# DMA transposes of whole tiles: one request for four blocks of 128 columns in place of four requests

## The chip, the cores and the metric

One core of a Trainium2 chip (trn2). The metric is the device time of one execution in microseconds (us). "Faster" or "slower" means by more than 2%.

## The reference, cut to what matters

The input x is 2048 rows of 512 columns. It is normalised by rows, goes through a local attention of 32 heads and, in parallel, through a gated MLP; the two results are multiplied and added to x.

```python
xn = _layernorm(x, axis=-1)                       # (1, 2048, 512)
s = _A_ref(xn, A_wqkv, A_wo)                      # xn @ wqkv (512 x 1536), attention, @ wo
g = _silu(_B_ref(xn, B_w_gate, B_w_up, B_w_down)) # 512 -> 1792 -> 512
return x + s * g
```

All first products contract over the 512 columns of xn, and the kernel's matmuls read xn with its columns on the partitions: each 128 x 512 tile of xn has to be transposed into four blocks of 128 x 128.

## The kernel before

The rows come in four stages of 512 (`TQ`), each of four tiles (`TPQ`). The first five tiles are transposed by TensorE; the other eleven by DMA, issued on SyncE (`nc.sync`), 44 requests of one block each:

```python
    def transpose_by_dma(t, cs=range(NC)):          # NC = 4 blocks in a tile
        j, i = divmod(t, TPQ)
        if i == 0 and 0 in cs:
            xnT[j] = xtp.tile([P, NC, TQ], BF16, name="xnT")
        for c in cs:
            nc.sync.dma_start(
                out=xnT[j][:, c, i * P : (i + 1) * P],
                in_=xns[t][:, c * P : (c + 1) * P],
                transpose=True,
            )

    def project(ps, w, lo, j, i0=0, n=TQ):          # who reads xnT
        for dk in range(NC):
            nc.tensor.matmul(
                ps,
                lhsT=w[:, dk, lo : lo + P],
                rhs=xnT[j][:, dk, i0 : i0 + n],
                start=(dk == 0),
                stop=(dk == NC - 1),
            )
```

A stage runs `glu` (gate and up projections, 14 times), then `qkv` of the *next* stage, then `down`, the sums of the attention, and the output. The transposes for a stage are issued a stage ahead, in what I call a train. SyncE also issues all loads and stores, in this order around the trains:

```python
    for i in range(TPQ):
        ...
        at(("glu", 1, 0) if i else ("down", 0, 3), transpose_by_dma, 2 * TPQ + i)   # second train
        ...
        at(("glu", 2, 0) if i else ("down", 1, 3), transpose_by_dma, 3 * TPQ + i)   # third train
    ...
    at(("glu", 0, 0), transpose, TPQ)                          # by TensorE
    at(("glu", 0, 0), transpose_by_dma, TPQ + 1, (0, 1))       # first train
    at(("glu", 0, 0), load_v, 0)                               # four loads of v_arr
    at(("glu", 0, 0), transpose_by_dma, TPQ + 1, (2, 3))
    at(("glu", 0, 0), transpose_by_dma, TPQ + 2)
    at(("glu", 0, 0), transpose_by_dma, TPQ + 3)
    at(("glu", 0, 0), load_late_weights)                       # wd, then wo
    for j in (2, 3):
        at(("glu", 0, 0), load_x, j * TPQ, TPQ)
```

The softmax here doesn't subtract the row's maximum and nothing guards it: scores larger than these inputs give would overflow.

Of the kernel before, what the change touches and what calls it, by code (L numbers as in the profile page):

```python
# [13 lines left out]
P = 128  # L14
# [14 lines left out]
def kernel(  # L29
# [13 lines left out]
    nc = tc.nc  # L43
# [71 lines left out]
    def load_late_weights():  # L115
# [18 lines left out]
        out=vT.rearrange("(k p) n -> p k n", p=P)[:, :, 0:PAD],  # L134
        in_=zpad[:],
# [34 lines left out]
    xnT = {}  # L170
# [35 lines left out]
    xns = {}  # L206
# [42 lines left out]
    def transpose_by_dma(t, cs=range(NC)):  # L249
        j, i = divmod(t, TPQ)  # L250
        if i == 0 and 0 in cs:
            xnT[j] = xtp.tile([P, NC, TQ], BF16, name="xnT")
        for c in cs:
            nc.sync.dma_start(
                out=xnT[j][:, c, i * P : (i + 1) * P],
                in_=xns[t][:, c * P : (c + 1) * P],
                transpose=True,
            )

    def project(ps, w, lo, j, i0=0, n=TQ):  # L260
        for dk in range(NC):
# [233 lines left out]
    for i in range(TPQ):  # L495
        at(("down", 0, 1), moments, 2 * TPQ + i)
        at(("down", 0, 2), normalize, 2 * TPQ + i)
        at(("glu", 1, 0) if i else ("down", 0, 3), transpose_by_dma, 2 * TPQ + i)
        at(("glu", 1, 10 + i), moments, 3 * TPQ + i)
        at(("qkv", 2, i), normalize, 3 * TPQ + i)  # L500
        at(("glu", 2, 0) if i else ("down", 1, 3), transpose_by_dma, 3 * TPQ + i)
# [100 lines left out]
    for n, fo in enumerate((0, 2, 4, 6, 8, 10)):  # L602
# [6 lines left out]
        copy_out(0, fo, ps[:], HQ, HQ, 2)  # L609
    at(("glu", 0, 0), transpose, TPQ)  # L610
    at(("glu", 0, 0), transpose_by_dma, TPQ + 1, (0, 1))
    at(("glu", 0, 0), load_v, 0)
    at(("glu", 0, 0), transpose_by_dma, TPQ + 1, (2, 3))
# [63 lines left out]
```

## Time and profile before

| | before |
|---|---|
| time, median | 227.72 us |
| TensorE busy, granted clock | 97% of the span, 0.999 |
| transposes on SyncE | 44 requests, 1.23 us each |
| first qkv matmul of stages 1, 2, 3 | 44.08, 97.93, 151.79 us |
| last transpose of its train landed | 43.63, 94.74, 147.42 us |

SyncE only issues here: its timeline before holds 126 DMA requests and, but for waits, nothing else. How long it is held by a request is the request's duration in its timeline (1.23 us, the median of the transposes); when the data are there is told by "landing" (2.4 us after the start, 12.0 at most). A transpose can cost kernel time if it lands after TensorE wants its tile (e4 shows it: landed at 45.56 us, TensorE's start at 45.60), or, as I thought and no run shows by itself, if SyncE, being held, issues something else too late. So the last two rows of the table are the ones to read together.

### The profile page before, as it was taken

To read this page: it belongs to the slowest core of one execution; us is meant where nothing else is said; L and a number is where in the kernel's file an instruction comes from. 1 tells how busy PE (TensorE), PEld (TensorE's weight loads), DVE (VectorE), ACT (ScalarE), POOL (GpSimd) and SP (SyncE) were. 2 spreads that over 40 slices of the span, in tenths; PEclk is the share of its full clock that TensorE was granted. 3 is DMA by queue.
4 is the path that set the end of the run, shared out by engine and by line. 5 is a ranking of instruction groups with operands and counts; after the bars stand their busy time and mean duration, and the time that the engine had idled before them with its cause. 6 is when DMAs were issued, how large, how long until landed. Compare 5 with 4: busy or idle time off the path is not lost.

```text
span 226.8 us, 3616 instructions
## 1 busy us (share of the span) xinstructions
PE 220.7 (97%) x1317; PEld 106.9 (47%) x1338; DVE 151.9 (67%) x281; ACT 131.9 (58%) x208; POOL 28.0 (12%) x67
## 2 busy tenths in 40 slices
PE   8899999999999999999999999999999999999994
PEld 4795444444444444444444444444444444444453
DVE  5588972999993589969821759934934348972334
ACT  4297669767631776676751476766763356755210
POOL 1025981000120000323700000000000000000000
PEclk9999999999999999999999999999999999999999
DMA  6998499399069911000239921100207950001001
GB/s 189 351 402 277 100 200 123 84 336 283 16 139 201 178 29 23 20 1 0 92 77 203 193 74 26 23 0 0 84 23 155 201 133 0 1 3 30 0 32 61
DMA packets 30770, 24.77 MB, mean 109 GB/s; under 512 B 11424, under 2 KB 30240, under 8 KB 30752
## 3 DMA queue, kind: packets, MB, share of 16 engines
q1 hardware_dynamic: 30752, 24.54, 45.7%
q8 instruction: 10, 0.16, 0.3%
q14 instruction: 8, 0.07, 0.1%
HBM read 18.74 MB, written 4.34 MB: 102 GB/s over the span
## 4 chain that ended last, share of the span: by engine, by line
PE 86%; DVE 6%; DMA 3%; ACT 1%; issue 1%; SPq 1%; ACTq 0%; DVEq 0%
PE u_ps L262 21%; PE y_ps L456 20%; PE g_ps L262 20%; PE qkv_ps L262 12%; PE s_ps L472 6%; DVE pk L333 3%; PE L_ps L351 3%; PE o_ps L419 3%; DMA x_sb<-in_A_x_dram 3%; ACT u L446 1%; DVE pv L405 1%; SPq L100 1%; DVE stats L187 1%; PE den_ps L371 0%; PE tr L220 0%
## 5 line engine op out<-in xcount | busy, mean ns | idle before, releaser
L262 PE MATMUL u_ps<-xnT,wu_sb 128*128 128x512 bf16 x220 | 57.1, 379 | 0.4
L262 PE MATMUL g_ps<-xnT,wg_sb 128*128 128x512 bf16 x218 | 56.5, 379 | 0.2
L456 PE MATMUL y_ps<-wd_sb,h 128*128 128x512 bf16 (+1 forms) x233 | 49.3, 366 | 0.2
L446 ACT ACTIVATE u<-u_ps 128x512 bf16<-128x512 f32 x56 | 33.5, 598 | 16.9 <-PE u_ps L262 16.6
L444 ACT ACTIVATE ge<-g_ps 128x512 bf16<-128x512 f32 x56 | 33.5, 598 | 16.9 <-PE g_ps L262 15.9
L405 DVE TENSOR_TENSOR pv<-E,v_arr 128x1024 bf16<-128x1024 bf16 (+1 forms) x48 | 39.9, 863 | 3.9 <-ACT ge L444 3.9
L333 DVE TENSOR_TENSOR pk<-q_sb,k_sb 128x1024 bf16<-128x1024 bf16 (+1 forms) x56 | 38.9, 762 | 4.6 <-ACT k_sb L286 4.6
L448 DVE TENSOR_TENSOR h<-ge,u 128x512 bf16<-128x512 bf16 x56 | 23.8, 424 | 23.7 <-ACT u L446 22.1
L262 PE MATMUL qkv_ps<-xnT,wqkv_sb 128*128 128x512 bf16 (+2 forms) x197 | 36.8, 344 | 0.2
L456 PEld LDWEIGHTS <-h 128*128 128x128 bf16 x238 | 23.1, 98 | 25.9 <-issue 1.3
L262 PEld LDWEIGHTS <-wu_sb 128*128 128x128 bf16 x224 | 21.9, 98 | 26.4
L262 PEld LDWEIGHTS <-wg_sb 128*128 128x128 bf16 x224 | 21.7, 98 | 26.6 <-issue 0.8
L464 ACT ACTIVATE sl<-y_ps 128x512 bf16<-128x512 f32 (+1 forms) x17 | 9.7, 572 | 32.3 <-PE y_ps L456 28.7
L262 PEld LDWEIGHTS <-wqkv_sb 128*128 128x128 bf16 x200 | 18.9, 98 | 17.5
L480 DVE TENSOR_TENSOR m<-s_ps,sl 128x512 bf16<-128x512 f32 (+1 forms) x17 | 11.1, 655 | 21.4 <-PE s_ps L472 21.4
L204 POOL TENSOR_TENSOR rstd<-rstd,mhalf 128x1 f32<-128x1 f32 x12 | 8.1, 671 | 72.0 <-DVE rstd L201 72.0
L431 DVE TENSOR_TENSOR oT<-o_ps,rb 128x1024 bf16<-128x1024 f32 x8 | 9.4, 1219 | 10.5 <-DMA rb<-rs_d 10.5
L472 PE MATMUL s_ps<-wo_sb,oT 128*128 128x512 bf16 (+1 forms) x65 | 14.6, 366 | 0.2
L286 ACT ACTIVATE vst<-qkv_ps 128x512 bf16<-128x512 f32 x14 | 8.4, 597 | 3.7 <-PE qkv_ps L262 3.7
L286 ACT ACTIVATE k_sb<-qkv_ps 128x512 bf16<-128x512 f32 x14 | 8.4, 601 | 3.2 <-PE qkv_ps L262 3.2
L286 ACT ACTIVATE q_sb<-qkv_ps 128x512 bf16<-128x512 f32 x14 | 8.3, 603 | 3.0 <-PE qkv_ps L262 3.0
L472 PEld LDWEIGHTS <-oT 128*128 128x128 bf16 x68 | 6.6, 98 | 7.2
(64 smaller groups left out, 134.6 us busy)
## 6 DMA issues: line engine op xcount, KB each, us to landing
v_arr<-vT SPq DMA_DIRECT2D x16, 520.0 KB, 8.5
vT<-vst SPq DMA_DIRECT2D x8, 256.0 KB, 2.2
out_dram<-o_t SPq DMA_DIRECT2D x15, 128.0 KB, 3.0
wg_sb<-in_B_w_gate_dram SPq DMA_DIRECT2D x2, 896.0 KB, 10.0
wu_sb<-in_B_w_up_dram SPq DMA_DIRECT2D x2, 896.0 KB, 11.2
wd_sb<-in_B_w_down_dram SPq DMA_DIRECT2D x1, 1792.0 KB, 8.0
wqkv_sb<-in_A_wqkv_dram SPq DMA_DIRECT2D x4, 384.0 KB, 5.8
x_sb<-in_A_x_dram SPq DMA_DIRECT2D x3, 512.0 KB, 7.7
```

The source lines that it names most:

```text
L262: nc.tensor.matmul(ps, lhsT=w[:, dk, lo : lo + P], rhs=xnT[j][:, dk, i0 : i0 + n], start=(dk == 0), stop=(dk == NC - 1),)
L286: nc.scalar.activation(out=dst, in_=ps, func=AF.Copy)
L333: nc.vector.tensor_tensor(out=st[j]["pk"][w][:, c0 : c0 + n, :], in0=st[j]["q"][:, c0 : c0 + n, :], in1=k_sb[j][:, c0 : c0 + n, off : off ...
L405: nc.vector.tensor_tensor(out=pv[:, d : d + n, :], in0=st[j]["E"][:, wh, :].unsqueeze(1).to_broadcast([P, n, TQ]), in1=st[j]["va"][:, 4 * ...
L431: nc.vector.tensor_tensor(out=oT[:, g : g + 2, :], in0=st[j]["o"][:, g : g + 2, :], in1=st[j]["rb"][:].unsqueeze(1).to_broadcast([P, 2, TQ ...
L444: nc.scalar.activation(out=ge[:], in_=g_ps[:], func=AF.Gelu_apprx_tanh)
L446: nc.scalar.activation(out=u[:], in_=u_ps[:], func=AF.Copy)
L448: nc.vector.tensor_tensor(out=h[:], in0=ge[:], in1=u[:], op=ALU.mult)
L456: nc.tensor.matmul(y[:], lhsT=st[j][fc][:, tt * P : (tt + 1) * P], rhs=wd_sb[:, fc, cols], start=(fc == 0), stop=(fc == NF - 1),)
L464: nc.scalar.activation(out=sl[:], in_=y[:], func=AF.Silu)
L472: nc.tensor.matmul(s[:], lhsT=st[j]["oT"][:, g, tt * P : (tt + 1) * P], rhs=wo_sb[:, g, cols], start=(g == 0), stop=(g == NC - 1),)
L480: nc.vector.tensor_tensor(out=m[:], in0=s[:], in1=sl[:], op=ALU.mult)
```

## The change

The intent: a tile's four blocks in one request, so that SyncE and the DMA queue handle a quarter of the requests.

```diff
-        for c in cs:
-            nc.sync.dma_start(
-                out=xnT[j][:, c, i * P : (i + 1) * P],
-                in_=xns[t][:, c * P : (c + 1) * P],
-                transpose=True,
-            )
+        nc.sync.dma_start(
+            out=xnT[j][:, cs[0] : cs[-1] + 1, i * P : (i + 1) * P],
+            in_=xns[t][:, cs[0] * P : (cs[-1] + 1) * P],
+            transpose=True,
+        )
```

## The prediction

With them went terms of the forecast's sum, namely how the hold of 1.23 us splits into a part per request and a part per block, which no trace of the kernel before can tell. The sum came to 3.3 us for a request of four blocks (1.9 for one of two), to 37 us of SyncE for all transposes in place of 54, and to 0 us on the path. The 1.9, 3.3 and 37 us, and what is made from them (a first train that ends at 35.5 us, wd at about 35, some 7 us earlier, later trains of 10 us), are the estimate; from the trace come only the bounds, 1.23 us if the hold is all per request and 4 x 1.23 = 4.9 if it is all per block.

What the trace before shows: its 126 requests land in the order in which they were issued. That semaphores are reused can be read there too: the requests use numbers 102 to 109 in turn, and the transpose that starts at 38.64 us has number 107, like the v_arr load eight requests earlier, which landed at 38.62.

> **What bounds the kernel now.** I read the page first (busy shares, slices, the chain that ended last), then the instructions that touch the tile that is transposed, then SyncE's timeline and waits, then TensorE's timeline at the three places where a transposed tile is first used. From the page:
>
> ```profile
> PE 220.7 (97%) x1317; PEld 106.9 (47%) x1338; DVE 151.9 (67%) x281; ACT 131.9 (58%) x208; POOL 28.0 (12%) x67
> ...
> PE   8899999999999999999999999999999999999994
> ...
> PE 86%; DVE 6%; DMA 3%; ACT 1%; issue 1%; SPq 1%; ACTq 0%; DVEq 0%
> ```
>
> TensorE (PE) is busy in every slice from the third to the last but one, at a granted clock of 0.999, and 86% of the chain is TensorE. The matmuls of 512 columns start every 0.216 us. Between 12.6 and 223.6 us I measured, from start to start, what each matmul takes beyond the usual spacing of its form: only steps of 0.22 us remain, each the size of one matmul whose record is missing, and about 0.1 us at each change to or from matmuls of 32 rows. So there is no real wait left on TensorE after 12.6 us: about 0.1 us is to be had there, no more. What lies before 12.6 us (loads of x and wqkv) has no DMA transpose in it. From the instructions on the tile xnT and from SyncE's timeline (start, duration, operation, count):
>
> ```profile
> L254 SPq DMA_TRANSPOSE xnT<-xn x44: 1104/1230/1933, 19.0 to 145.0; - x44
> DMA to landing us min/median/max: 2.2/2.4/12.0
> ...
> 24.14 2.83 SPq L307 DMA_DIRECT2D v_arr<-vT  x4
> 27.02 15.50 SPq L254 DMA_TRANSPOSE xnT<-xn  x10
> 42.56 0.58 SPq L116 DMA_DIRECT2D wd_sb<-in_B_w_down_dram  x1
> ...
> 66.24 5.07 SPq L254 DMA_TRANSPOSE xnT<-xn  x4
> 72.62 5.43 SPq L483 DMA_DIRECT2D out_dram<-o_t  x4
> 78.51 15.12 SPq L254 DMA_TRANSPOSE xnT<-xn  x12
> ...
> 130.44 15.84 SPq L254 DMA_TRANSPOSE xnT<-xn  x12
> ```
>
> The 44 requests hold SyncE 1.23 us each, in three trains of 12 to 16 requests. TensorE first needs the tiles of a train at the first qkv matmul of the next stage (start, duration, operation):
>
> ```profile
> 43.21 1.03 PE L262 MATMUL u_ps<-xnT,wu_sb 128*128 128x512 bf16 x4
> 44.08 2.10 PE L262 MATMUL qkv_ps<-xnT,wqkv_sb 128*128 128x512 bf16 x9
> ...
> 97.07 1.03 PE L262 MATMUL u_ps<-xnT,wu_sb 128*128 128x512 bf16 x4
> 97.93 1.24 PE L262 MATMUL qkv_ps<-xnT,wqkv_sb 128*128 128x512 bf16 x5
> ...
> 150.93 1.03 PE L262 MATMUL u_ps<-xnT,wu_sb 128*128 128x512 bf16 x4
> 151.79 1.46 PE L262 MATMUL qkv_ps<-xnT,wqkv_sb 128*128 128x512 bf16 x6
> ```
>
> None of the three waits: each starts 0.86 us after the group before it, as four matmuls of 0.216 us do. The last requests of the trains start at 41.29, 92.41 and 145.05 us and land 2.34, 2.34 and 2.37 us later, at 43.63, 94.74 and 147.42. The margins are thus 0.45, 3.2 and 4.4 us. The transposes are hidden, the first train only just.
>
> [...] a lone request lands after 2.3 us, while requests that had queued up land about 0.21 us apart (78.07, 78.29, 78.51, 78.72). [...] transposes issued from 27 us on land from 39.05 us, after the last v_arr load at 38.62. [...] (who waited <- for whom: us, times, longest):
>
> ```profile
> SPq L483 <- DMA v_arr<-vT: 3.6, 2, 2.6
> ...
> SPq L254 <- DMA v_arr<-vT: 1.9, 2, 1.6
> ```
>
> A transpose does not read v_arr. It waits because completion semaphores are reused in turn, every eighth request: the instruction order shows lanes 0 to 7, and each of these waits is for the request eight places earlier.
>
> **The change part by part.** The order of instructions shows the same program on TensorE, VectorE, ScalarE and GpSimd. On SyncE, 44 transposes become 12: two of two blocks (the first tile that is split around the v_arr load) and ten of four blocks. The bytes are the same.
> - Removed: 32 requests. If the whole 1.23 us were per request, SyncE would gain 32 x 1.23 = 39 us. If it were all per block, nothing. [...] I take 3.3 us, between 1.3 and 4.9.
> - Also removed: waits for lanes. After the first v_arr load, the 2-, 4- and 4-block requests come within eight places of the loads and wait for VectorE alone; the wait for v_arr moves to the loads of wo behind them, which nobody needs before 70 us.
> - Moved: the first train ends near 27.0 + 1.9 + 3.3 + 3.3 = 35.5 us on SyncE in place of 42.5. It still lands behind the v_arr load of 38.62, ten blocks at 0.2 to 0.4 us each: at 41 to 42.6 us in place of 43.63. The load of wd starts at about 35 in place of 42.56 and is wanted at 54.4. The trains from 78.51 and 130.44 last 10 us in place of 15.
> - What of it is on the path: nothing. The path there is TensorE matmuls back to back; the margin of 0.45 us grows to some 2 us, and a larger margin is worth nothing. The sum is 0 us, and the time stays at 227.7.
>
> **The rivals.**
> (a) The whole-tile form is slower per block. Against it: the bytes are the same and the form is plain. For it: no trace here has the form, its destination is four runs per partition, 512 elements apart. How slow must it be? With x us of SyncE per block and 1.1 us from the end of the issue to landing (2.33 - 1.23), the trains are late by 10x - (44.08 - 1.1 - 27.02) = 10x - 16.0, by 12x - (97.93 - 1.1 - 78.51) = 12x - 18.3 and by 12x - (151.79 - 1.1 - 130.44) = 12x - 20.3. All are zero up to x = 1.5. The sum of 34x - 54.6 reaches 2% (4.55 us) at x = 1.74, 41% above today's 1.23. At twice the cost per block, 2.46 us, the kernel would be 29 us slower. I give 3% to anything beyond 2%.
> (b) The wd load, now some 7 us earlier, runs into the last v_arr load. VectorE waits for that load (3.94 us of idle time before the first pv; the load lands at 38.62):
>
> ```profile
> 34.38 0.43 DVE L448 TENSOR_TENSOR h<-ge,u 128x512 bf16<-128x512 bf16 x1 [1.30 <-ACT u L446]
> 38.74 1.22 DVE L405 TENSOR_TENSOR pv<-E,v_arr 128x2048 bf16<-128x2048 bf16 x1 [3.94 <-ACT ge L444]
> ```
>
> The bracket names ScalarE, but E was done at 36.75 us; the load is what ended the wait. From there VectorE is busy to 59.23 us with work that the logits at 59.40 need, so each us that the load loses beyond some 0.2 to 1 us comes out of TensorE. For it: 1.8 MB join the queue. Against it: [...]the last v_arr load took 12.43 and 12.20 us with transposes behind it against 11.09 us in the last stage without. Worth 0 to +1 us.
> (c) A gain: a train's end on the path. It would need TensorE to wait now, and it doesn't. Worth -0.1 us at most; more than 2% is out of reach, since all non-TensorE time after 12.6 us is smaller than that.
>
> **Range and chances.** The three runs of before span 0.15 us; another chip may shift all by a few tenths (the estimate of (b) adds up to +1, (c) takes 0.1). I predict 227.7, 8 in 10 between 227.1 and 228.5. Faster by over 2% (under 223.2): 1%. Slower by over 2%: 3%. Within 2%: 96%.
>
> **What would show it.** Right: 12 transposes of 2 to 4.9 us on SyncE, ten of them near 3.3; the last of the first train landed before 43 us; first qkv matmuls still 0.86 us behind the group before; TensorE busy time within 0.5 us of 220.7; no SyncE wait of a transpose for v_arr. Wrong: a wait of TensorE for xnT before a qkv group (rival a), or for pk before the logits, with the first pv later than 38.74 us (rival b).

## The result, and the profile after

The changed kernel took 227.70 us (227.44 to 227.92, six runs) against 227.72 us (227.51 to 228.04, six runs) before: ratio 0.9997, 95% interval 0.9984 to 1.001, the same. Ratios here are the mean time of one kernel's fast runs over that of the other's fast runs of the same rounds, so not quite the ratio of the medians quoted.

From the page of the changed kernel, the busy shares and the chain that ended last:

```profile
PE 221.9 (98%) x1338; PEld 107.4 (48%) x1338; DVE 151.9 (67%) x281; ACT 131.8 (58%) x208; POOL 22.0 (10%) x67
...
PE 98%; DVE 0%; issue 0%; DVEq 0%
```

The chain is now called TensorE alone. That looks like an improvement and is none: the trace before lacked the records of 21 matmuls (1317 of 1338), which left holes through which the chain can step into other engines (e10, the kernel before with fewer transposes and a whole trace, has TensorE at 96%). SyncE, in contrast, has changed a lot. First the instructions on xnT (duration in ns: min/median/max), then SyncE's timeline (start, duration, operation, count):

```profile
L253 SPq DMA_TRANSPOSE xnT<-xn x12: 1188/1266/3272, 18.3 to 131.9; - x12
```

```profile
23.05 2.77 SPq L306 DMA_DIRECT2D v_arr<-vT  x4
25.87 7.27 SPq L253 DMA_TRANSPOSE xnT<-xn  x3
33.19 0.59 SPq L116 DMA_DIRECT2D wd_sb<-in_B_w_down_dram  x1
33.82 6.35 SPq L119 DMA_DIRECT2D wo_sb<-in_A_wo_dram  x4
...
65.09 2.89 SPq L253 DMA_TRANSPOSE xnT<-xn  x1
71.89 3.51 SPq L482 DMA_DIRECT2D out_dram<-o_t  x4
75.45 3.81 SPq L253 DMA_TRANSPOSE xnT<-xn  x3
...
129.31 3.84 SPq L253 DMA_TRANSPOSE xnT<-xn  x3
```

Three requests of four blocks each take 3.81 us together, where twelve requests of one block took 15.12. Behind freshly issued v_arr loads the request is held longer: 2.89 us, and 3.27 us for the longest. The view of SyncE's waits puts the long holds of the first train down to VectorE, but this is no wait for data: those requests read only tiles of xn, the last of which was written by 19.71 us. The trains now land at 38.74, 80.36 and 134.79 us. TensorE's first use of them in stages 1 and 2:

```profile
42.48 1.03 PE L261 MATMUL u_ps<-xnT,wu_sb 128*128 128x512 bf16 x4
43.34 2.97 PE L261 MATMUL qkv_ps<-xnT,wqkv_sb 128*128 128x512 bf16 x13
...
96.34 1.03 PE L261 MATMUL u_ps<-xnT,wu_sb 128*128 128x512 bf16 x4
97.20 1.03 PE L261 MATMUL qkv_ps<-xnT,wqkv_sb 128*128 128x512 bf16 x4
```

The step is 0.86 us in both, as before; the margins have grown from 0.45, 3.2 and 4.4 us to 4.6, 16.8 and 16.3 us (43.34 - 38.74, 97.20 - 80.36, 151.06 - 134.79). A larger margin buys nothing.

The profiled spans differ by 0.74 us (226.83 and 226.09), which tempts one to see a gain. To separate it I measure in each trace **the stretch**: from the start of the first matmul of `qkv_ps` to the start of TensorE's last instruction. It is 210.72 us before and 210.72 us after. Of the 0.74 us, 0.73 lie ahead of it: the first `qkv_ps` starts at 12.46 us before and at 11.73 after, before any DMA transpose has been issued. In the experiments below that start varies from 11.47 to 12.48 us whatever the kernel, so I put it down to the loads of the start (the last wqkv load lands at 10.35 us before and at 9.31 after). The stretch does not, so it resolves what the times can't.

### The profile page after: what moved, and what is told of

The parts are those of the page before. It is cut to its first block, busy times and chain, and to the rows that moved or that the text cites. A ratio compares the mean times of both kernels' runs of the same rounds, so it can differ in the third digit from the quotient of the medians.

```text
span 226.1 us, 3600 instructions
## 1 busy us (share of the span) xinstructions
PE 221.9 (98%) x1338; PEld 107.4 (48%) x1338; DVE 151.9 (67%) x281; ACT 131.8 (58%) x208; POOL 22.0 (10%) x67
## 4 chain that ended last, share of the span: by engine, by line
PE 98%; DVE 0%; issue 0%; DVEq 0%
PE y_ps L455 22%; PE g_ps L261 21%; PE u_ps L261 21%; PE qkv_ps L261 16%; PE s_ps L471 6%; PE L_ps L350 3%; PE o_ps L418 3%; PE qk_ps L547 2%; PE v_ps L547 1%; PE warm_ps L244 1%; PE qk_ps L538 1%; PE den_ps L370 0%; PE v_ps L538 0%; PE tr L220 0%; PE trb L220 0%; DVE m L479 0%
## 5 line engine op out<-in xcount | busy, mean ns | idle before, releaser
L261 PE MATMUL g_ps<-xnT,wg_sb 128*128 128x512 bf16 x224 | 57.5, 379 | 0.0
L455 PE MATMUL y_ps<-wd_sb,h 128*128 128x512 bf16 (+1 forms) x238 | 49.9, 367 | 0.0
L443 ACT ACTIVATE ge<-g_ps 128x512 bf16<-128x512 f32 x56 | 33.5, 598 | 16.9 <-PE g_ps L261 16.8
```

The lines of the kernel that those rows point to most:

```text
L261: nc.tensor.matmul(ps, lhsT=w[:, dk, lo : lo + P], rhs=xnT[j][:, dk, i0 : i0 + n], start=(dk == 0), stop=(dk == NC - 1),)
L443: nc.scalar.activation(out=ge[:], in_=g_ps[:], func=AF.Gelu_apprx_tanh)
L455: nc.tensor.matmul(y[:], lhsT=st[j][fc][:, tt * P : (tt + 1) * P], rhs=wd_sb[:, fc, cols], start=(fc == 0), stop=(fc == NF - 1),)
```

## The experiments

Ten kernels in eleven runs (e9, one request for two tiles, did not build with this layout of xnT). Each ratio is to the kernel before, on the same chip (before: medians 227.75 to 227.78 us). "Small transpose" means 16 rows x 128 columns into a spare tile of 32 bytes per partition. The record marks all eleven as correct, and that says little: e10 reads wrong tiles, and it passes too. The product that is added to x is too small (an estimate from random numbers of the reference's scales: 0.000014 beside 0.05), so the check hardly sees what the transposes write. The times stand; that the whole-tile request puts every block in its place is not shown by this check.

### e4: two more requests in the first train, kernel before

```diff
+    def extra(t):
+        for c in range(2):
+            again = spare.tile([P, 16], BF16, name="again")
+            nc.sync.dma_start(out=again[:], in_=xns[t][0:16, c * P : (c + 1) * P], transpose=True)
     at(("glu", 0, 0), transpose_by_dma, TPQ + 2)
+    at(("glu", 0, 0), extra, TPQ + 2)
     at(("glu", 0, 0), transpose_by_dma, TPQ + 3)
```

> The kernel before, with two further small transposes (16 rows x 128 columns into a spare tile) issued on SyncE between the third and the fourth tile of the first train. Theory (the transposes are hidden, and in the first train only by 0.45 to 1.1 us): the second of them is the eighth request after the last v_arr load and waits for its landing near 38.6 us, the four blocks of the fourth tile follow at 1.27 us each, the last starts near 43.8 in place of 41.3 us, and TensorE waits at the first qkv group of the second stage: 1.4 to 2.1 us slower, 229.1 to 229.9 us. Rival (SyncE's requests never reach the path, or small requests hold it for nothing): 227.7 us.

Measured: 229.16 us, ratio 1.0054 (1.0040 to 1.0068), under the 2% but clear of noise; the stretch is 212.06 us, 1.34 more. SyncE's timeline, then TensorE's:

```profile
34.78 4.58 SPq L619 DMA_TRANSPOSE again<-xn  x2
39.46 5.00 SPq L255 DMA_TRANSPOSE xnT<-xn  x4
```

```profile
43.62 1.10 PE L263 MATMUL qkv_ps<-xnT,wqkv_sb 128*128 128x512 bf16 x3
45.60 2.75 PE L263 MATMUL qkv_ps<-xnT,wqkv_sb 128*128 128x512 bf16 x12 [0.89 <-DMA xnT<-xn]
```

The second small request starts at 38.24 us, just after the last v_arr load landed (38.23), though it reads nothing of v_arr: the wait is for the request eight places earlier, as in the kernel before (38.64 and 38.62 us). The last block lands at 45.56 us, and TensorE's fourth matmul, which reads it, starts at 45.60. So in the kernel before the first train had less room than two requests, and running out of it costs time at once. The time lies in the range expected, the 1.34 us just below the 1.4 to 2.1: counted from the first `qkv_ps`, the last request starts 2.40 us later than in the kernel before, where 2.5 were expected.

### e5: the same two requests, changed kernel

The edit is that of e4.

> The same two further requests at the same place in the changed kernel. Theory: the first train has some 4.6 us to spare there (last landing 38.74 against 43.34 us), so no change: 227.7 us, within 0.3. Rival (the margin of the changed kernel is no larger, because the data wait behind the v_arr load anyway): 229 us or more, as with the kernel before.

Measured: 227.61 us, ratio 0.9993 (0.9979 to 1.0006); the stretch is 210.72 us. The last transpose lands at 39.23 us, well before the first qkv matmul. The same load that costs the kernel before 0.5% costs the changed one nothing. The change did create room, and the rival, that the v_arr load takes it away again, is out.

### e2: a small transpose behind every request, kernel before

```diff
                 transpose=True,
             )
+            again = spare.tile([P, 16], BF16, name="again")
+            nc.sync.dma_start(out=again[:], in_=xns[t][0:16, c * P : (c + 1) * P], transpose=True)
```

> The kernel before with a small transpose (16 rows x 128 columns into a spare tile) behind each of its 44 requests. Theory (SyncE pays per request, and the trains are hidden only up to their margins): if a small request holds SyncE for about 1.23 us as a block does, the last landing of the three trains is late by about 10, 11 and 9 us, each seen as a wait of TensorE before a qkv group: about 258 us (250 to 265). If the hold goes with the bytes, a small one costs an eighth, 0.15 us, and only the first train is late, by 1 to 2 us: about 229 us. Rival (requests never reach the path): 227.7 us.

Measured: 270.77 us, ratio 1.1871 (1.1824 to 1.1918). In four fences: who waited for whom on TensorE (us in total, times, longest); the instructions on the spare tile (ns); TensorE's granted clock in 40 slices; TensorE's timeline at the end of the first train:

```profile
PE qkv_ps L267 <- DMA xnT<-xn: 32.0, 12, 5.1
```

```profile
L261 SPq DMA_TRANSPOSE again<-xn x44: 1087/1222/2204, 19.4 to 190.8; - x44
```

```profile
PEclk9999999559999999955999999996589999999999
```

```profile
55.55 8.72 PE L267 MATMUL qkv_ps<-xnT,wqkv_sb 128*128 128x512 bf16 x30 [2.02 <-DMA xnT<-xn]
```

A request with an eighth of the bytes holds SyncE for 1.22 us, as a whole block does. The mechanism is as expected, twelve waits of TensorE for xnT at the three qkv groups, but the size is not: +42.4 us in the stretch (253.14 - 210.72) where I had some +30. From start to start the late matmuls exceed their usual 0.216 us by 11.64, 12.04 and 12.25 us, together 35.9; each train is later than I had worked out, by 1 to 3 us. The other 6.5 us are a term that I had left out: after the waits of each train eleven matmuls are slow, nine of them 0.427 us apart and not 0.216. The granted clock reads 5 tenths around these waits, whose longest is 5.1 us (0.63 on average from 42 to 58 us, the first train, and 0.77 from 58 to 62), and the slow matmuls fill 4.5 to 4.6 us each time. What takes the clock down and brings it back, these runs don't tell. So in e2 the late transposes cost TensorE more than their lateness, 42.4 us against 35.9; in e4, whose wait was 0.89 us, no matmul was slowed.

### e3: a small transpose behind every request, changed kernel

The edit is that of e2, once for each of the 12 requests.

> The changed kernel with a small transpose behind each of its 12 requests. Theory: 24 requests of about 1.3 us (2.5 to 3.3 us while the v_arr loads fill the queue) stay within the margins of all three trains: 227.7 us, within 0.4. If the whole-tile form had gained no room it would go up as the kernel before does.

Measured: 227.88 us, ratio 1.0003 (0.9990 to 1.0017); the stretch is 210.72 us. TensorE has no wait for xnT. Note that it got 12 further requests and e2 got 44: the comparison shows what a rule of "one more request for each" costs the two forms, not equal loads. Equal loads are e4 and e5.

### e1: two blocks per request

```diff
-        nc.sync.dma_start(
-            out=xnT[j][:, cs[0] : cs[-1] + 1, i * P : (i + 1) * P],
-            in_=xns[t][:, cs[0] * P : (cs[-1] + 1) * P],
-            transpose=True,
-        )
+        for c in range(cs[0], cs[-1] + 1, 2):
+            nc.sync.dma_start(
+                out=xnT[j][:, c : c + 2, i * P : (i + 1) * P],
+                in_=xns[t][:, c * P : (c + 2) * P],
+                transpose=True,
+            )
```

> Requests of two blocks: 22 in place of 44 or 12. Time 227.7 us, within 0.4, by every theory. The hold of SyncE by a request that finds the queue empty tells the per-request share: one block took 1.23 and four took 1.26 us, so if all of it is per request, two take 1.23 to 1.26 us[...].

Measured: 227.73 us, ratio 0.9994 (0.9978 to 1.0010); the stretch is 210.72 us. The instructions on xnT in the second train, where the v_arr loads are out of the way (duration ns: min/median/max): one block per request (kernel before), two (e1), four (changed kernel):

```profile
L254 SPq DMA_TRANSPOSE xnT<-xn x12: 1104/1230/1237, 78.5 to 92.4; - x12
```

```profile
L254 SPq DMA_TRANSPOSE xnT<-xn x6: 1167/1240/1246, 75.4 to 81.8; - x6
```

```profile
L253 SPq DMA_TRANSPOSE xnT<-xn x3: 1188/1257/1265, 75.5 to 78.0; - x3
```

With 1.22 us for the small one of e2, that is 1.22, 1.23, 1.24 and 1.26 us for an eighth, one, two and four blocks: the hold is per request, and about 0.01 us per block. All per block would have been 2.46 us for two (2 x 1.23); the prediction's estimate was 1.9 for two and 3.3 for four.

### e6: the v_arr loads behind the first transpose of the next stage

```diff
-        if j + 1 < NJ:
-            load_v(j + 1)
+    for j in range(NJ - 1):
+        at(("down", j, 3), load_v, j + 1)
```

> The changed kernel with the v_arr loads of stages 1 to 3 issued behind the first whole-tile transpose of the next stage, not ahead of it. In the changed kernel that transpose held SyncE for 2.9 and 2.7 us with v_arr loads queued, against 1.2 to 1.3 us otherwise. Theory (the queue's fill stretches the hold): it falls to about 1.27 us. Rival (four blocks cost about 2.8 us by themselves, and the short ones are special): it stays near 2.8. Time: the v_arr loads start some 3 to 8 us later and land close to the first pv of their stage; 227.7 us, at most 1 us more.

Measured: 228.19 us, ratio 1.0014 (0.9997 to 1.0030), the same; the stretch is 210.73 us. The first whole-tile request of the second train, in the changed kernel and in e6 (duration in ns):

```profile
L253 SPq DMA_TRANSPOSE xnT<-xn x1: 2892/2892/2892, 65.1 to 65.1; - x1
```

```profile
L253 SPq DMA_TRANSPOSE xnT<-xn x1: 1239/1239/1239, 64.1 to 64.1; - x1
```

With no load queued ahead, the hold falls from 2.89 to 1.24 us (in the third train from 2.66 to 1.21). So the long holds need the loads ahead of them. But there the blocks count too: right behind the loads of the second train the first request was held for 1.22 us with one block (kernel before), 1.85 with two (e1) and 2.89 with four; in the third train for 1.27, 1.86 and 2.66 us. In this one place the prediction's estimate (1.9 us for two, 3.3 for four) comes near. Pending loads alone are not enough, though: in e5 the fourth tile's request took 1.21 us at 31.91 us, and the last v_arr load landed only at 36.98. And it is not peculiar to transposes: the first wo load was held for 4.42 us in the changed kernel. What a request waits for there, I did not find out. It delays nothing that is wanted soon.

### e10: no transposes in the second and third train, kernel before

```diff
         j, i = divmod(t, TPQ)
+        if j > 1:
+            xnT[j] = xnT[j - 2]
+            return
```

> The kernel before without any transpose in the second and third train: stages 2 and 3 read the tiles of stages 0 and 1 again, so the result is wrong on purpose. 32 of 44 requests are gone and no landing can be late. This is more than any change to these requests can save. Theory (hidden): 227.7 us, within 0.4. Rival (they cost time in some way that the chain does not show, by their DMA traffic or by putting off SyncE's other requests): below 227 us.

Measured: 227.99 us, ratio 1.0007 (0.9991 to 1.0022); the stretch is 210.72 us. Even taking 32 of the 44 requests away altogether saves nothing. This bounds what any change to those requests could gain here.

### e8: the fifth tile by DMA too

```diff
-    at(("glu", 0, 0), transpose, TPQ)
+    at(("glu", 0, 0), transpose_by_dma, TPQ)
```

> The changed kernel with the fifth tile too transposed by one whole-tile request in place of four TensorE transposes and a copy on ScalarE. It takes four matmuls of 128 columns, 0.22 us, off TensorE, which is the bound, and puts one request of 1.27 us ahead of the others on SyncE, where there is room before the v_arr load. If every TensorE instruction after 12.6 us is on the path: 0.2 us faster (0.1%), 227.5 us. Rival: the v_arr load is put off and VectorE with it: up to 1 us slower.

Measured: 227.52 us, ratio 0.9989 (0.9978 to 1.0001). TensorE's timeline at the place in the changed kernel, then in e8:

```profile
17.00 0.39 PE L220 MATMUL tr<-ident,xn 128*128 128x128 bf16 x4
17.23 1.03 PE L261 MATMUL g_ps<-xnT,wg_sb 128*128 128x512 bf16 x4
```

```profile
16.95 1.03 PE L261 MATMUL g_ps<-xnT,wg_sb 128*128 128x512 bf16 x3
```

The four transposes between the last `qkv_ps` and the first `g_ps` are gone, and the stretch is 210.50 us, 0.22 less, the size of the work removed. The interval of the times touches 1, so by time alone it is not settled; the trace shows it. This is the use of the room on SyncE: moving work off the engine that bounds. Its stretch is the shortest, by 0.1%.

### e7: all four tiles of the first train in one request each, ahead of the v_arr load

```diff
-    at(("glu", 0, 0), transpose, TPQ)
-    at(("glu", 0, 0), transpose_by_dma, TPQ + 1, (0, 1))
-    at(("glu", 0, 0), load_v, 0)
-    at(("glu", 0, 0), transpose_by_dma, TPQ + 1, (2, 3))
-    at(("glu", 0, 0), transpose_by_dma, TPQ + 2)
-    at(("glu", 0, 0), transpose_by_dma, TPQ + 3)
+    for i in range(TPQ):
+        at(("glu", 0, 0), transpose_by_dma, TPQ + i)
+    at(("glu", 0, 0), load_v, 0)
```

> As the former, with all four tiles of the first train in one request each, ahead of the v_arr load rather than around and behind it. SyncE needs 4 x 1.27 = 5.1 us from about 18.3 us, so the load goes from 23.05 to about 24 us; with no transposes behind it the fourth load should land after 11 to 11.5 us in place of 12.4, so about when it did. Time 227.5 us (0.2 less than before). Rival: the load lands over 1 us later and VectorE's work with it: 228 us or more.

Measured: 227.74 us, ratio 0.9998 (0.9983 to 1.0012); the stretch is 210.96 us, so the 0.22 us were won and 0.46 us lost. The last v_arr load took 13.39 us (12.38 in the changed kernel) and landed at 39.34 us; the wd load is issued right behind it. VectorE's first pv, in e7:

```profile
39.47 1.23 DVE L404 TENSOR_TENSOR pv<-E,v_arr 128x2048 bf16<-128x2048 bf16 x1 [5.82 <-ACT ge L443]
```

The rest of VectorE's work in that stage shifts with it, its last pk ends near 59.9 us, and the logits' matmuls wait for it (2.36 us for them in place of 1.90). My expectation that the load would land after 11 to 11.5 us failed. So a late v_arr load does reach TensorE, on the path that rival (b) of the prediction names. What made it late is not shown by this run: it took 1.01 us longer, but it was also issued 1.06 us later than in the changed kernel, counted from the first `qkv_ps`.

### e12 and e11: e7 again, and with the wd load put off

e11 is e7 with six small transposes between the v_arr and the wd load; e12 is e7 unchanged, as its control, one run of 227.40 us.

```diff
     at(("glu", 0, 0), load_v, 0)
+    at(("glu", 0, 0), hold, TPQ + 3, 6)      # six small transposes
     at(("glu", 0, 0), load_late_weights)
```

> The kernel with all four transposes ahead of the v_arr load once more, as a control for the next run on the same chip. In its first profile the last v_arr load, with the wd load queued right behind it, took 13.39 us (12.38 in the changed kernel), the first pv began at 39.47 us, and TensorE lost 0.46 us before the logits of stage 1: from its first qkv_ps matmul to its last instruction 210.96 us, where 210.50 were to be had. The same again, within 0.1, if that is the order of requests and not chance.

> The same kernel with six small transposes into a spare tile between the v_arr load and the wd load, so that the wd load is issued about 34 to 35 us in place of 26.7. Theory (the wd load, queued right behind, slows the last v_arr load: rival b of the prediction): the last v_arr load lands after 11.4 to 12.4 us, the first pv begins about 1 to 2 us earlier than in the control, the wait before the logits is gone, and the stretch from the first qkv_ps matmul to the last instruction of TensorE is 210.50 us. Rival (it is only that the v_arr load is issued 0.9 us later): the landing stays at 13.4 us and the stretch at 210.96.

Measured: e11 227.84 us, ratio 1.0007 (0.9987 to 1.0027). With wd issued at 35.48 in place of 26.45 us, the last v_arr load took 12.64 us against 13.30 in the control: 0.66 us less, part of the way back. But in this run SyncE issued that load 0.96 us later (26.55 against 25.59), so it landed no earlier, and the wait did not go: stretch 210.66 against 210.55 us. Neither expectation held whole, and the control missed its own: its load took about as long as in e7, but its stretch is not within 0.1 us of 210.96. That the wd load right behind it slows the v_arr load is thus suggested and not shown: with it, the load took 13.39 (e7) and 13.30 us (e12); without it, 12.28 to 12.86 us in ten profiles, but 13.22 in e1, where wd was issued only at 32.85 us. What is consistent is the threshold. In the three runs, the load landed 27.42 (e12), 27.53 (e11) and 27.82 us (e7) after the first `qkv_ps`, and the stretch exceeded 210.50 us by 0.05, 0.16 and 0.46 us: each is the landing less 27.37, to 0.01. Where TensorE still does the fifth tile's transposes its own work is 0.22 us later, so the threshold there is about 27.6 us, and the load lands at 26.2 us before and at 25.8 us after. VectorE thus has some 1.4 us to spare before and 1.8 after, estimated from these numbers.

## Why the prediction was right, and what in it was wrong

- **No wait of TensorE is left to remove**: right. The stretch is 210.72 us before, after, and without two thirds of the requests (e10); and the trace after, which lacks no matmul's record, has no step over 0.38 us from one matmul to the next after 12.6 us.
- **The transposes are hidden, the first train only just**: right. Two more requests in the first train reach the path (e4, +1.34 us); in the changed kernel they don't (e5).
- **A whole-tile request holds SyncE for 3.3 us**: wrong in size. With no loads ahead it is 1.26 us, nearly all of it per request, just under even the wide range of 1.3 to 4.9; it is 2.5 to 3.3 us only behind loads (e1, e6). So the sign "ten of them near 3.3" failed. The estimate failed because it put over half of the 1.23 us on the block without a measurement: the trace before has requests of one block alone and could not tell. Had it been on the path, the sum would have been wrong too: SyncE's twelve transposes took 21.4 us and not 37. The time could not tell, since no hold was on the path: that it came out right speaks for the margins and not for this estimate.
- **The trains**: SyncE's part of the first ended at 33.1 us (35.5 said); it landed at 38.74 us, 1.25 us after the last v_arr load, so earlier than the 41 to 42.6 said, and the later trains last 3.8 us, not 10. All err on the harmless side.
- **The wait for v_arr moves from the transposes to the wo loads**: half right. No transpose waits for v_arr any more. But the wo loads don't either: the semaphore of the first one was free once the v_arr load eight places earlier had landed, at 28.71 us, and it was issued at 33.82; SyncE's waits name v_arr nowhere. It was then held for 4.42 us all the same (33.82 to 38.24), and in e7 for 10.38 us with its semaphore free since 24.29. This is the hold behind loads of e6, whose cause is open.
- **Rival (a), slower per block**: refuted; a train of twelve blocks takes a quarter of the time.
- **Rival (b), the earlier wd load slows v_arr**: it did not happen in this change (12.38 against 12.43 us, first pv 25.88 us after the first `qkv_ps` against 26.28). A late v_arr load does cost time (e7); that the wd load makes it late is not shown (e11). The prediction's case against it left a number out: beside 12.43 and 12.20 us with transposes behind, the third stage's load took 11.56. The slack that I gave VectorE, 0.2 to 1 us, is about 1.4.
- **TensorE busy within 0.5 us of 220.7**: missed; 221.9 is 0.7 above that band, for the dull reason that the trace before lacked 21 records.

## What to carry to other kernels

A DMA transpose here holds SyncE for 1.2 us per request when no loads are ahead of it, whether it moves an eighth of a block or four blocks, so ask for the most that one request can express; but look first at when the data land and when they are first read, because off the path the saving is room and not time. Room can then be spent: on moving work off the engine that bounds (e8), or on surviving a schedule with more requests (e5). And measure a hidden change by a stretch between two fixed instructions of the bounding engine: it repeated within 0.01 us where the time of the kernel before varied by 0.7 (227.5 to 228.2).
